# Decay products of a chunk in one scan, tokens and router scores from one matmul, and chunk rows laid six to each eight partitions

## The chip, the core and the metric

The kernel runs on one core of a Trainium2 chip. Such a core has a matrix engine (TensorE, PE in the profile, with its weight load PEld in a row of its own), a vector engine (VectorE, DVE), an activation engine (ScalarE, ACT), a general engine (GpSimd, POOL) and an engine that only issues transfers (SyncE, SP). They run side by side and wait for each other through semaphores. Each works through its own instructions in the order in which the program lists them, so an instruction that waits holds up everything behind it on its engine. Data lies in 128 partitions of on-chip memory. Matmul results land in a second memory, PSUM. Sixteen DMA engines carry data between DRAM and the chip.

The metric is device time in microseconds (us). The kernel before the change took 320.49 us, the median of three runs (319.43 to 320.95).

## What is computed

Two stages follow each other. The first is linear attention with a decay (RWKV) over 4 batches of 8 heads, 768 tokens and 48 features a head; the second is a mixture of 8 experts over the 3072 rows of 384 values that the first one writes. Every row goes to one expert, and a row whose skip score is not positive stays as it is.

```
for t in range(S):                       # per batch and head, D = 48
    cur = einsum('bhd,bhe->bhde', u * k_t, v_t)
    y_t = einsum('bhd,bhde->bhe', r_t, state + cur)
    state = w_t[..., None] * state + einsum('bhd,bhe->bhde', k_t, v_t)
x = y as (3072, 384)
skip = x @ w_skip > 0 ;  e = argmax(x @ w_gate) ;  g = softmax weight of e
out = x + g * relu(x @ w1[e]) @ w2[e]    # rows with skip, else out = x
```

## The kernel before

The tokens of a batch are cut into 6 chunks of 128, so there are 24 chunks in all (batch outermost). Heads are handled in pairs: partitions 0 to 47 hold the 48 features of an even head, partitions 64 to 111 those of the odd one, and a free axis `a` of length 4 counts the pairs. Partitions 48 to 63 and 112 to 127 hold zeros.

The recurrence is turned into matrix products. For each chunk `prep_scan` makes q, the product of the decays from a token to the chunk's end, by a scan that runs backwards over the tokens (line 261); a scan is an instruction in which each element is made from the one before it, here state = max(w * state, floor). `prep_keys` makes rh, the product from the chunk's start divided by the whole product (a reciprocal on line 271, then forward scans that start from it, line 276), and kq = k * q on POOL (line 274). `prep_reads` makes rp = r * rh on DVE (line 284) and rk = r * k on POOL (line 287). Each kind of scan takes four instructions, one for each head pair, since a new pair has to start afresh.

The matmuls of a chunk are: `intra` transposes kq into kt (line 306) and forms the 128 x 128 scores psA (line 313), which `mask` multiplies by a triangle on DVE (line 319, two instructions); `bonus_sums` and `bonus` give the term with u (lines 328 and 332); `update` adds kt and v to the state in psu (line 341), which `carry` scales and copies on ACT (lines 351 and 356); `outputs` sums the chunk's result in psY, from the masked scores (line 363) and, from the second chunk of a batch on, from the state (line 368); `evict` copies it to xT on ACT (line 373). `rows_out` turns xT into rows of tokens by four transposes (line 379), and makes the 9 router scores by four more matmuls with 9 columns (line 381). `store` copies scores and rows out on ACT (lines 389 and 391) and issues the transfer to `out`.

The main loop goes over steps s = -2 to 24. In step s the chunk s is finished (update, outputs, rows_out), chunk s+1 gets its scores, and chunk s+2 its scans; the rows of chunk s-1 are stored, and the loads of chunk s+4 are issued. Tile order is written out by hand (`manual_schedule`), so the code's order is each engine's order. After 6, 12, 18 and 24 chunks a router pass over the finished rows is spread over the next steps, a few small DVE instructions at a time (`drip`); for the first two passes ACT also makes `hot` tables in three steps (lines 462 and 463, called marks below). Beside that, the first experts' weights are loaded and split into a high and a low part, the high one on ACT (line 106), the low one on POOL (line 266). The second stage starts after the last router pass and is not touched by the change.

A chunk's w, r and k arrive by two transfers of 48 partitions each (line 152), one for each half of the partitions, into one of three buffers; v with tokens along the free axis comes in two more (line 154), and v with tokens in partitions in one (line 159). For the first chunk the host has laid out 128 rows with zeros between the halves, and three transfers bring them (lines 144 to 146). The zeros of the two other buffers are written by DVE (line 203) and POOL (line 215) before the loads are issued.

## Time and profile before

| | |
|---|---|
| median of three runs | 320.49 us (319.43 to 320.95) |
| the profiled execution's own time | 320.93 us |
| its span in the trace | 319.1 us, so 1.8 us lie around it |
| first stage up to the last chunk's copy of psY | about 166 us |
| PE, DVE, ACT, POOL busy | 94%, 76%, 58%, 37% of the span |
| moved by DMA | 60.48 MB |

The trace is of one execution. Its views give, for each instruction, a start in us from the span's start, a duration, and where an engine sat idle before it, what ended the idle time. A row that groups instructions ends with the time the group was busy and the mean duration of one in ns. Durations of instructions that follow each other on one engine overlap by some hundredths of a us, so the distance from one start to the next is a better cost than the duration.

### The profile page before, as it was taken

The page shows a single profiled execution, that of the slowest core. Times are in us where ns is not written, and L with a number is a line of the kernel's source. Part 1 is how long each engine was busy: PE and PEld are TensorE (multiplying, and loading weights), DVE is VectorE, ACT ScalarE, POOL GpSimd, SP SyncE. Part 2 cuts the span into 40 slices and gives each one's busy share as a digit, 9 for nine tenths or more (in the row PEclk, how much of TensorE's full clock was granted, in tenths as well). Part 3 has the DMA queues.
Part 4 walks back from the last instruction along what each step waited for, and adds up shares of the span by engine and source line. Part 5 has one row for each costly group of instructions (what it writes and reads, how often), then busy time and mean ns, then how long its engine had stood idle before and what let it go on. Part 6 is the DMA issues. An engine that isn't in the chain of part 4 may idle for free.

```text
span 319.1 us, 8696 instructions
## 1 busy us (share of the span) xinstructions
PE 299.8 (94%) x3325; PEld 280.0 (88%) x3325; DVE 243.2 (76%) x573; ACT 184.4 (58%) x503; POOL 116.6 (37%) x118
## 2 busy tenths in 40 slices
PE   6399999999999999989999999999999999999991
PEld 2289998889788987979889899999999999999991
DVE  7789899999999999999626369587685949596310
ACT  4327765869876898756734258375573818284200
POOL 7164345655455556543401674311102020101111
PEclk9969999999999999979999999999999999999997
DMA  7999999999899998884410479865656373630000
GB/s 228 243 213 226 176 267 276 267 263 264 219 239 234 267 212 179 189 196 165 128 41 25 122 255 359 285 228 197 230 197 238 129 259 99 243 147 26 8 15 25
DMA packets 23108, 60.48 MB, mean 189 GB/s; under 512 B 4102, under 2 KB 10666, under 8 KB 23056
## 3 DMA queue, kind: packets, MB, share of 16 engines
q1 hardware_dynamic: 20576, 53.69, 61.9%
q0 software_dynamic: 2048, 5.48, 5.1%
q8 instruction: 28, 0.46, 0.6%
q10 hardware_dynamic: 432, 0.66, 0.6%
q14 instruction: 24, 0.20, 0.2%
HBM read 52.76 MB, written 7.86 MB: 190 GB/s over the span
## 4 chain that ended last, share of the span: by engine, by line
PE 76%; DVE 9%; DMA 8%; ACT 2%; issue 1%; POOL 1%; SPq 0%; ACTq 0%; POOLq 0%; DVEq 0%
PE psO L768 7%; PE psO L766 7%; PE psO L767 7%; PE psH L748 6%; PE psH L747 6%; PE psH L746 6%; PE psY L363 6%; PE psB L328 6%; PE psA L313 6%; PE psY L368 5%; DMA wrk<-wrk 4%; PE psH L125 4%; DVE asb L319 3%; PE psX L381 3%; DMA vt<-wrk 3%; PE psT L306 2%
## 5 line engine op out<-in xcount | busy, mean ns | idle before, releaser
L753 ACT ACTIVATE hh<-psH 128x256 fp32r<-128x256 f32 x60 | 23.1, 384 | 55.7 <-PE psH L748 52.4
L710 POOL DMA_INDIRECT out<-fin,ids x16 | 16.9, 1058 | 101.5 <-DVE fin L773 93.3
L748 PE MATMUL psH<-xTh,w1l 128*128 128x256 f32 x168 | 47.5, 283 | 0.0
L747 PE MATMUL psH<-xTl,w1h 128*128 128x256 f32 x168 | 47.5, 283 | 0.0
L746 PE MATMUL psH<-xTh,w1h 128*128 128x256 f32 x168 | 47.5, 283 | 0.0
L276 DVE TENSOR_TENSOR_SCAN rh<-wrk,rh,pss 128x127 f32<-128x127 f32 x96 | 38.1, 459 | 3.6 <-ACT tab L503 1.1
L766 PE MATMUL psO<-w2h,hh 128*128 128x384 f32 x120 | 40.7, 339 | 0.0
L768 PE MATMUL psO<-w2h,hl 128*128 128x384 f32 x120 | 40.1, 334 | 0.0
L767 PE MATMUL psO<-w2l,hh 128*128 128x384 f32 x120 | 40.1, 334 | 0.0
L287 POOL TENSOR_TENSOR rk<-wrk 128x512 f32<-128x512 f32 x24 | 30.6, 1275 | 24.7 <-DVE rp L284 16.6
L274 POOL TENSOR_TENSOR kq<-wrk,q 128x512 f32<-128x512 f32 x24 | 28.3, 1181 | 21.8 <-PE psu L341 7.3
L319 DVE TENSOR_TENSOR asb<-psA,c_sb 128x512 f32<-128x512 f32 x48 | 30.8, 682 | 6.5 <-PE psA L313 6.4
L363 PE MATMUL psY<-asb,v 128*48 128x128 f32 x384 | 26.8, 284 | 8.6 <-DVE psY L332 8.4
L754 DVE SCALAR_TENSOR_TENSOR hl<-psH,hh 128x256 fp32r<-128x256 f32 x60 | 25.2, 420 | 12.5 <-ACT hh L753 12.1
L261 DVE TENSOR_TENSOR_SCAN q<-wrk,pss 128x128 f32<-128x128 f32 x96 | 32.3, 398 | 2.7 <-DMA wrk<-wrk 2.7
L748 PEld LDWEIGHTS psH<-xTh,w1l 128*128 128x128 f32 x168 | 32.2, 192 | 0.0
L747 PEld LDWEIGHTS psH<-xTl,w1h 128*128 128x128 f32 x168 | 32.2, 192 | 0.0
L746 PEld LDWEIGHTS psH<-xTh,w1h 128*128 128x128 f32 x168 | 32.2, 191 | 0.0
L773 DVE SCALAR_TENSOR_TENSOR fin<-psO,gates,xg 128x384 f32<-128x384 f32 x15 | 9.3, 618 | 28.5 <-PE psO L768 28.5
L363 PEld LDWEIGHTS psY<-asb,v 128*48 128x48 f32 x384 | 20.8, 127 | 9.8 <-DVE psY L332 9.7
L95 DVE TENSOR_TENSOR w2l<-r,w2h 128x512 fp32r<-128x512 f32 x42 | 27.8, 687 | 1.0
L328 PE MATMUL psB<-rk,ubk_sb 128*128 128x128 f32 x192 | 28.0, 289 | 0.3 <-POOL rk L287 0.3
(145 smaller groups left out, 682.0 us busy)
## 6 DMA issues: line engine op xcount, KB each, us to landing
r<-w SPq DMA_DIRECT2D x48, 512.0 KB, 5.7
wrk<-wrk SPq DMA_DIRECT2D x46, 288.9 KB, 5.9
v<-vN SPq DMA_DIRECT2D x24, 192.0 KB, 5.6
out<-x SPq DMA_DIRECT2D x24, 192.0 KB, 5.2
vt<-wrk SPq DMA_DIRECT2D x46, 96.0 KB, 5.7
wrk<-wrk SPq DMA_DIRECT2D x1, 258.5 KB, 3.7
wrk<-wrk ACTq DMA_DIRECT2D x1, 256.0 KB, 3.9
wrk<-wrk SPq DMA_DIRECT2D x1, 256.0 KB, 4.5
```

Source lines behind the costliest of these rows:

```text
L261: ins = nc.vector.tensor_tensor_scan(q[:, a, :P][:, ::-1], w4[:, a, :P][:, ::-1], floor.to_broadcast([P, P]), 1.0, op0=ALU.mult, op1=ALU.max)
L276: nc.vector.tensor_tensor_scan(rh[:, a, 1:], wk["w4"][:, a, :P - 1], zero.to_broadcast([P, P - 1]), rh[:, a, 0:1], op0=ALU.mult, op1=ALU.max)
L287: mul = nc.gpsimd.tensor_tensor(rk.rearrange("p a j -> p (a j)"), wk["w"][:, R_OFF:K_OFF], wk["w"][:, K_OFF:V_OFF], op=ALU.mult)
L319: nc.vector.tensor_tensor(s, psa[g], tri.rearrange("p (o j) -> p o j", o=1).to_broadcast([P, NP, P]), op=ALU.mult)
L328: nc.tensor.matmul(wk["psb"][:, a], ubk_sb[:, a], wk["rk"][:, a], start=True, stop=True)
L363: nc.tensor.matmul(psy[64 * g:64 * g + D, a], v[:, 2 * a + g], wk["asb"][g][:, a], start=False, stop=(c == 0), skip_group_check=True)
L746: nc.tensor.matmul(ps, w1h[:, o:o + P], xTh[:, kc], start=(kc == 0), stop=False)
L747: nc.tensor.matmul(ps, w1h[:, o:o + P], xTl[:, kc], start=False, stop=False)
L748: nc.tensor.matmul(ps, w1l[:, o:o + P], xTh[:, kc], start=False, stop=(kc == KC - 1))
L766: nc.tensor.matmul(pso, h[j, fc][0], w2h[:, o], start=(fc == 0), stop=False)
L767: nc.tensor.matmul(pso, h[j, fc][0], w2l[:, o], start=False, stop=False)
L768: nc.tensor.matmul(pso, h[j, fc][1], w2h[:, o], start=False, stop=(fc == FC - 1))
```

## The change

**Layout.** A chunk's 48 rows of a head half now lie six to each eight partitions. One transfer brings all 128 partitions: its source pattern takes 16 groups, each six rows further on, and of each group eight rows, so that partitions 6 and 7 of every eight hold a copy of the next group's first two rows. The last chunk, whose last group would read past the array's end, takes two transfers. The copies must not count, so a column `own` (1 in the six, 0 in the two) is made from the identity matrix by a DVE reduction at the start. It scales u (line 255) and the reciprocal rq (line 303, a new ACT instruction in every chunk), and with that the read side rp is zero in those partitions. The clearing of two load buffers goes.

**Whole scans.** q and rh are now one scan of 516 elements each. The four rows of 129 hold a zero decay at the joint, and the scan's second operand is a mask in PSUM (1.0 at the joints, 1e-30 elsewhere, 16-bit values) in place of one broadcast number. rh starts from 1, and the division moves into rp: four DVE instructions (line 316), one for each pair, multiply r, rq and rh, where one instruction multiplied r and rh before.

**Joined output matmul.** The four transposes and four 9-column matmuls of `rows_out` become four matmuls of 105 columns, whose fixed operand holds an identity of 96 columns and the 9 router columns. Their router columns overlap in pairs, so that the scores come as two halves: `store` copies 18 numbers, the rows in two ACT copies of 192 columns in place of one of 384, and the router adds the halves (one more DVE instruction in each pass). The state update's stationary operand grows from 48 to 64 columns.

**Order on POOL.** The low half of a weight slice (line 290 now) was tied to the first scan of the step; it is now tied to the last router instruction that DVE was given, if there was one.

```diff
-            for g in range(2):
-                nc.sync.dma_start(t[64 * g:64 * g + D], wrk[b, c, g, :, :V_OFF])
+            def rows(eng, o, m):
+                if i == n - 1:
+                    src = wrk[b, c].rearrange("g d x -> (g d) x")
+                    pat = [[6 * RW, 15], [RW, 8], [1, m]]
+                    eng.dma_start(t[120:126, o:o + m], src[90:, o:o + m])
+                    p = 120
+                else:
+                    pat, p = [[6 * RW, 16], [RW, 8], [1, m]], P
+                at = wrk[b, c, 0, :, o:o + m]
+                eng.dma_start(t[:p, o:o + m], bass.AP(at.tensor, at.offset, pat))
...
+            rows(nc.sync, 0, V_OFF)
...
-            nc.vector.memset(wrk_sb[1], 0.0)
-            nc.vector.memset(floor, Q_MIN)
-            nc.vector.memset(zero, 0.0)
+            nc.vector.memset(smask, Q_MIN)
+            nc.vector.memset(smask[:, :, 0:1], 1.0)
+            nc.vector.tensor_copy(smaskb, smask.rearrange("p a j -> p (a j)"))
+            nc.vector.tensor_copy(pss[:, 200:200 + NP * CW // 2], smaskb.bitcast(F32))
...
-            nc.gpsimd.memset(wrk_sb[2], 0.0)
...
+            nc.vector.tensor_reduce(own, ident.rearrange("p (i j) -> p i j", j=8)[:, :, :6],
+                                    axis=mybir.AxisListType.XY, op=ALU.add)
...
-            for a in range(NP):
-                ins = nc.vector.tensor_tensor_scan(
-                    q[:, a, :P][:, ::-1], w4[:, a, :P][:, ::-1], floor.to_broadcast([P, P]), 1.0,
-                    op0=ALU.mult, op1=ALU.max)
-                if a == 0 and lows:
-                    lo, raw, hi = lows.pop(0)
-                    beside(nc.gpsimd.tensor_tensor(lo, raw, hi, op=ALU.subtract), ins)
+            if lows:
+                lo, raw, hi = lows.pop(0)
+                mul = nc.gpsimd.tensor_tensor(lo, raw, hi, op=ALU.subtract)
+                if vec.last is not None:
+                    beside(mul, vec.last)
+            nc.vector.tensor_tensor_scan(
+                q.rearrange("p a j -> p (a j)")[:, ::-1], t[:, 1:1 + NP * CW][:, ::-1], floor, 0.0,
+                op0=ALU.mult, op1=ALU.max)
...
-            nc.vector.reciprocal(rh[:, :, 0:1], wk["q"][:, :, 0:1])
+            nc.vector.reciprocal(rq0, wk["q"][:, :, 0:1])
+            nc.scalar.activation(rq, rq0, AF.Copy, scale=own)
...
-            for a in range(NP):
-                nc.vector.tensor_tensor_scan(
-                    rh[:, a, 1:], wk["w4"][:, a, :P - 1], zero.to_broadcast([P, P - 1]),
-                    rh[:, a, 0:1], op0=ALU.mult, op1=ALU.max)
+            nc.vector.tensor_tensor_scan(
+                rh.rearrange("p a j -> p (a j)"), wk["w"][:, 0:NP * CW], floor, 0.0,
+                op0=ALU.mult, op1=ALU.max)
...
-            last = nc.vector.tensor_tensor(rp, wk["r"], rh, op=ALU.mult)
+            for a in range(NP):
+                last = nc.vector.scalar_tensor_tensor(
+                    rp[:, a], wk["r"][:, a], wk["rq"][:, a], wk["rh"][:, a, :P],
+                    op0=ALU.mult, op1=ALU.mult)
...
             for a in range(NP):
-                nc.tensor.transpose(psx[:, a, :LO], xT[:LO, a], ident[:LO, :LO])
-            for a in range(NP):
-                nc.tensor.matmul(psx[:, NP - 1, LO:LO + E + 1], xT[:, a], wgp_sb[:, a, 2 * D:],
-                                 start=(a == 0), stop=(a == NP - 1))
+                o = (a // 2) * X2 + (a % 2) * 2 * D
+                nc.tensor.matmul(px[:, o:o + XW], xT[:, a], wgp_sb[:, a], start=(a == 0),
+                                 stop=(a == NP - 1), skip_group_check=True)
...
-            nc.scalar.copy(x, psx.rearrange("p a (g d) -> p a g d", g=2)[:, :, :, :D])
+            for o in range(2):
+                nc.scalar.copy(x[:, o::2].rearrange("p h g d -> p h (g d)"),
+                               p2[:, :, o * XW:o * XW + 2 * D])
...
+            vec.tensor_tensor(lg, l2[:, :, 0], l2[:, :, 1], op=ALU.add)
```

Three places show how instructions stand now. The first is DVE in a step of the first batch, from the scans of chunk 3 to the bonus of chunk 2 (a scan is printed as SCALAR_TENSOR_TENSOR; the numbers behind a name count buffers). Before:

```order
L261 SCALAR_TENSOR_TENSOR q_117<-wrk_83,pss 128x128 x4
L271 RECIPROCAL rh_391<-q_117 128x4
L276 SCALAR_TENSOR_TENSOR rh_391<-wrk_83,rh_391,pss 128x127 x4
L284 TENSOR_TENSOR rp_399<-wrk_83,rh_391 128x512
L319 TENSOR_TENSOR asb_2_428<-psA_108,c_sb 128x512
L319 TENSOR_TENSOR asb_2_430<-psA_109,c_sb 128x512
L332 TENSOR_TENSOR psY<-psB_432,vt_88 128x512
```

And the same place on DVE in the changed kernel:

```order
L294 SCALAR_TENSOR_TENSOR q_375<-wrk_83,pss 128x516
L302 RECIPROCAL rq_390<-q_375 128x4
L308 SCALAR_TENSOR_TENSOR rh_395<-wrk_83,pss 128x516
L316 SCALAR_TENSOR_TENSOR rp_397<-wrk_83,rq_389,rh_395 128x128 x4
L353 TENSOR_TENSOR asb_2_429<-psA_112,c_sb 128x512
L353 TENSOR_TENSOR asb_2_431<-psA_113,c_sb 128x512
L366 TENSOR_TENSOR psY<-psB_433,vt_88 128x512
```

Eight scans became two and one product became four; the four read rq_389, which ACT writes.

The second place is ACT in a step of that batch: the stored rows, the state's carry, and the copies behind them. Before:

```order
L389 COPY lgs_356<-psX_441 128x9
L391 COPY x_457<-psX_441 128x384
L351 ACTIVATE psu<-psu,q_117 128x48 x4
L356 COPY sblk_111<-psu 64x4x48 x2
L373 COPY xT_502<-psY 128x512
L308 COPY kt_509<-psT_504 128x512
```

And ACT there in the changed kernel:

```order
L424 COPY lgs_355<-psX_442 128x18
L427 COPY x_453<-psX_442 128x2x96 x2
L385 ACTIVATE psu<-psu,q_375 128x48 x4
L390 COPY sblk_115<-psu 64x4x48 x2
L303 ACTIVATE rq_485<-rq_486,own 128x4
L407 COPY xT_500<-psY 128x512
L342 COPY kt_507<-psT_502 128x512
```

The new rq stands behind the whole carry, and the copy of the rows is in two parts.

The third place is DVE at the program's start, ahead of the first chunk's scans. Before:

```order
L208 MEMSET q_117 128x4
L210 MEMSET psA_108 128x512
L210 MEMSET psA_109 128x512
L261 SCALAR_TENSOR_TENSOR q_116<-wrk_83,pss 128x128 x4
L271 RECIPROCAL rh_182<-q_116 128x4
```

And in the changed kernel:

```order
L237 COPY pss<-smaskb 128x258
L239 MEMSET psA_112 128x512
L239 MEMSET psA_113 128x512
L251 TENSOR_REDUCE own<-c_sb 128x1
L294 SCALAR_TENSOR_TENSOR q_181<-wrk_83,pss 128x516
L302 RECIPROCAL rq_184<-q_181 128x4
```

The reduction that makes `own` reads the constants c_sb and stands ahead of the first scan.

More of the change, by code (lines that the diff above doesn't have):

```diff
@@ L46 @@
 XW = 2 * D + E + 1
+X2 = XW + 2 * D
 BIG = 65536.0
@@ L166, in rwkv_moe_kernel @@
         u_sb = keep.tile([P, NP], F32, name="u_sb")
+        u8_sb = pers.tile([P, NP], F32, name="u8_sb")
+        own = pers.tile([P, 1], F32, name="own")
         ident = c_sb[:, C_ID:C_ID + P]
@@ L191, in rwkv_moe_kernel, with __getattr__, issue @@
         pr = pss[:, :NC * E].rearrange("p (c e) -> p c e", e=E)
-        floor = pss[:, 500:501]
-        zero = pss[:, 501:502]
+        floor = pss[:, 200:200 + NP * CW // 2].bitcast(BF16)
         pt = pss[:, 64:64 + 2 * NV * E].rearrange("p (j q e) -> p j q e", j=2, q=NV)
-        qs = [pers.tile([P, NP, CW], F32, name=f"q{i}") for i in range(2)]
+        class Steps:
+            last = None
+            def __getattr__(self, name):
+                def issue(*a, **kw):
+                    self.last = getattr(nc.vector, name)(*a, **kw)
+                    return self.last
+                return issue
+        vec = Steps()
         def setup():
@@ L340, in update @@
                 for g in range(2):
-                    nc.tensor.matmul(psu[64 * g:64 * g + D, a, :D],
-                                     work[i]["kt"][:, a, 64 * g:64 * g + D],
+                    nc.tensor.matmul(psu[64 * g:64 * g + HP, a, :D],
+                                     work[i]["kt"][:, a, 64 * g:64 * g + HP],
                                      v_sb[i][:, 2 * a + g, :D],
@@ L432, in router @@
             sm = t("sm", 1)
-            nc.vector.tensor_reduce(sm, ex, axis=AX, op=ALU.add)
+            vec.tensor_reduce(sm, ex, axis=AX, op=ALU.add)
             yield 1
-            nc.vector.tensor_scalar(sm, sm, 1e-9, None, op0=ALU.add)
+            vec.tensor_scalar(sm, sm, 1e-9, None, op0=ALU.add)
             yield 1
             gate = t("gate", 1)
-            nc.vector.reciprocal(gate, sm)
+            vec.reciprocal(gate, sm)
             vals = att.tile([P, NC, NV, 1], BF16, tag="vals", name=f"vals{i0}")[:, :m]
@@ L466, in router @@
             last = i0 + m == n
-            small = nc.vector if last else nc.gpsimd
+            small = vec if last else nc.gpsimd
             for c in range(m):
@@ L525, in early @@
             yield 1
-            nc.vector.tensor_reduce(gate0, tab[:, 0, 2:NV, 0], axis=AX, op=ALU.add)
+            vec.tensor_reduce(gate0, tab[:, 0, 2:NV, 0], axis=AX, op=ALU.add)
             yield 1
@@ L686, in rwkv_moe_kernel @@
         psf = ps1.tile([P, 512], F32, tag="psT", name="psf", bufs=2)
-        nc.tensor.matmul(psf[0:1, 0:1], rows1, vt[:, 0:1], start=True, stop=False)
+        nc.tensor.matmul(psf[0:1, 0:1], rows1_, vt[:, 0:1], start=True, stop=False)
         nc.tensor.matmul(psf[0:1, 0:1], rows1_, vt[:, 2:3], start=False, stop=True)
```

70 lines of the change are left out of this document (39 added, 31 removed).

## The prediction

> **What bounds the kernel now.** I read the slices first, then the chain of work, then the instructions of two steps in order of time. In the 40 slices of 8 us the two engines that matter are these:
>
> ```profile
> PE   6399999999999999989999999999999999999991
> DVE  7789899999999999999626369587685949596310
> ```
>
> The first stage fills slices 1 to 21, and there both stand at 9. From about 168 us on PE alone is full, and the change touches nothing there. So two engines run close together, and which of them ends last has to be read step by step. The chain has this step in the first batch:
>
> ```profile
> 36.18 0.49 PE psu L341 x16
> 36.68 0.88 PE psY L363 x16
> 37.55 1.09 PE psY L368 x8
> 38.64 0.44 PE psT L306 x4
> 39.08 1.02 PE psA L313 x24
> 40.10 1.09 PE psB L328 x8
> 41.19 0.38 PE psX L379 x4
> 41.57 0.81 PE psX L381 x8
> ```
>
> The parts add to 6.20 us with no gap: PE is the bound in these steps, some six of them up to 54 us. Later the router's small instructions come on DVE and the marks on ACT. This is DVE over one later step, by starts, and the busy time in two stretches:
>
> ```profile
> 67.17 1.34 DVE L261 TENSOR_TENSOR_SCAN q<-wrk,pss 128x128 f32<-128x128 f32 x4
> 68.55 0.18 DVE L271 RECIPROCAL rh<-q 128x4 f32<-128x4 f32 x1
> 68.77 1.59 DVE L276 TENSOR_TENSOR_SCAN rh<-wrk,rh,pss 128x127 f32<-128x127 f32 x4
> 70.39 0.69 DVE L284 TENSOR_TENSOR rp<-wrk,rh 128x512 f32<-128x512 f32 x1
> 71.00 1.28 DVE L319 TENSOR_TENSOR asb<-psA,c_sb 128x512 f32<-128x512 f32 x2
> 72.20 0.69 DVE L332 TENSOR_TENSOR psY<-psB,vt 128x512 f32<-128x512 f32 x1
> 72.80 1.35 DVE L261 TENSOR_TENSOR_SCAN q<-wrk,pss 128x128 f32<-128x128 f32 x4
> ...
> core 0: us, PE busy (x) PEld busy (x) DVE busy (x) ACT busy (x) POOL busy (x), PEclk, DMA share, GB/s
> ...
> 70.00:80.00 10.00, 10.00 (x162) 9.26 (x157) 9.86 (x22) 9.71 (x28) 5.53 (x7) 1.00 1.03 256
> ...
> 130.00:140.00 10.00, 8.95 (x134) 7.86 (x135) 9.68 (x30) 6.62 (x22) 4.74 (x5) 0.88 0.75 172
> ```
>
> One chunk costs DVE 1.38 + 0.22 + 1.62 + 0.61 + 1.20 + 0.60 = 5.63 us from the first row to the last, and router instructions come on top. So from 54 us on DVE is the bound in the router's steps, and in the steps with marks (70 to 80) ACT is as full as DVE.
>
> **PE: the joined matmul.** Lines 379 and 381 take 0.38 + 0.81 = 1.19 us. Four matmuls with the same stationary size and 105 columns lie between the 0.81 us of four with 9 columns and the 1.09 us of four with 128 (line 328). By the columns between these ends that is 0.81 + 96/119 x 0.28 = 1.04, so PE saves 0.15 us a step (bounds 0.10 and 0.38). The wider stationary operand of line 341 (64 columns for 48) I cost at nothing, since 16 instructions in 0.49 us are 31 ns each and the 64-column ones of line 313 cost no more than 1.02/24 = 43 ns; at worst 16 x 12 ns = 0.19 us.
>
> **DVE: scans against products.** The mean durations of the groups:
>
> ```profile
> L276 DVE TENSOR_TENSOR_SCAN rh<-wrk,rh,pss 128x127 f32<-128x127 f32 x96 | 38.1, 459 | 3.6 <-ACT tab L503 1.1
> L754 DVE SCALAR_TENSOR_TENSOR hl<-psH,hh 128x256 fp32r<-128x256 f32 x60 | 25.2, 420 | 12.5 <-ACT hh L753 12.1
> L773 DVE SCALAR_TENSOR_TENSOR fin<-psO,gates,xg 128x384 f32<-128x384 f32 x15 | 9.3, 618 | 28.5 <-PE psO L768 28.5
> L261 DVE TENSOR_TENSOR_SCAN q<-wrk,pss 128x128 f32<-128x128 f32 x96 | 32.3, 398 | 2.7 <-DMA wrk<-wrk 2.7
> ```
>
> No scan of 516 is in the trace. From below: a DVE instruction on 4 elements takes 0.18 us (line 271 above), so a scan's slope is at least (398 - 181)/124 = 1.75 ns an element, and 516 take 1.08 us. From above: no fixed part at all, and the whole scan costs what the four do, 1.38. I take 1.19, nearer to the lower end because a fixed part is seen in every short row. That saves 0.19 us on q and 1.62 - 1.19 = 0.43 on rh (bounds 0 to 0.30, and 0.24 to 0.54). The mask as second operand costs nothing here: the old floor was read from PSUM as well.
>
> Against this, rp becomes four products with a factor per partition. Such a factor costs 459 - 398 = 61 ns in the scans. With it line 773 takes 618 ns for 384, without it line 754 takes 420 for 256, so the slope is (618 - 61 - 420)/128 = 1.07 ns, and 128 elements with a factor take 420 - 137 + 61 = 344 ns. Of that some 0.08 overlaps with the next (0.69 lasts, 0.61 to the next start), so four take 1.05 us where one took 0.61: 0.44 more. The bounds are 0 (four pack as closely as one) and 4 x 0.344 - 0.61 = 0.77 (no overlap). Together DVE saves 0.19 + 0.43 - 0.44 = **0.18 us a chunk** (bounds 0.84 saved and 0.53 lost). The addition of the score halves costs 0.2 in each router pass.
>
> **ACT and the new wait.** rp now waits for rq from ACT, where it stands behind the carry. In a step with marks:
>
> ```profile
> 74.26 0.48 ACT L391 COPY x<-psX 128x384 f32<-128x384 f32 x1
> ...
> 74.63 1.20 ACT L351 ACTIVATE psu<-psu,q 128x48 f32<-128x48 f32 x4
> ...
> 75.61 1.18 POOL L274 TENSOR_TENSOR kq<-wrk,q 128x512 f32<-128x512 f32 x1
> ...
> 75.86 0.64 ACT L356 COPY sblk<-psu 64x192 f32<-64x192 f32 x2
> 76.02 1.31 DVE L284 TENSOR_TENSOR rp<-wrk,rh 128x512 f32<-128x512 f32 x1
> ...
> 77.25 1.28 DVE L319 TENSOR_TENSOR asb<-psA,c_sb 128x512 f32<-128x512 f32 x2
> ```
>
> The carry ends at 76.50. rq lasts 0.19 at most (as the reciprocal does on DVE), and the split copy costs between nothing more and 0.64 - 0.37 = 0.27 (the two 192-element copies of line 356, against 74.63 - 74.26); I take 0.08. With two such copies and one earlier rq ahead of it, rq is done near 76.95. rp then takes 1.05 and ends at 78.0, where today the next instruction starts at 77.25 (rp lasts 1.31 there, through the end of kq on POOL). So such a step loses 0.75 us, and behind rp the masks, the bonus and PE's line 363 are queued. A second such step adds 0.2 by the same drift: 0.95 for a batch, two batches with marks, **1.9 us lost**. In the PE-bound steps the wait is covered: psA, which the masks need, ends at 40.10, which is 3.9 us after psu begins, and carry, rq and rp together (0.5 for the store, 1.2, 0.64, 0.2, 1.05) end 3.6 after it. If that cover went, masks would come late by the difference.
>
> **Start.**
>
> ```profile
> 1.18 0.45 ACTq L147 DMA_DIRECT2D c_sb<-cst  x1
> ...
> 4.52 1.36 DVE L261 TENSOR_TENSOR_SCAN q<-wrk,pss 128x128 f32<-128x128 f32 x4 [0.60 <-DMA wrk<-wrk]
> ...
> 10.67 1.36 DVE L261 TENSOR_TENSOR_SCAN q<-wrk,pss 128x128 f32<-128x128 f32 x4 [2.09 <-DMA wrk<-wrk]
> ...
> 16.45 0.88 PE L363 MATMUL psY<-asb,v 128*48 128x128 f32 x6 [4.96 <-DVE psY L332]
> ...
> c_sb<-cst ACTq DMA_DIRECT2D x1, 128.0 KB, 4.7
> ```
>
> `own` makes the first scan wait for c_sb, until 1.18 + 4.7 = 5.9, and takes some 0.3: the scan starts 1.7 us later. The idle 2.09 us ahead of the second chunk's scan covers it. From there to PE's first psY it is 5.78 us now, and 1.19 + 0.22 + 1.19 + 1.05 + 1.80 = 5.45 then, and chunk 1 may land sooner without the cleared buffer. I take 0.6 us gained (bounds 1.0 lost, 0.9 gained).
>
> **The sum**, against the profiled execution's 320.93 us: start -0.6; six PE-bound steps x 0.15 = -0.9; about ten chunks under DVE x 0.18 less three additions of 0.2 = -1.2; marks +1.9; three PE-bound steps near 150 us -0.45. The last router pass gains 0.15 from the shorter psX and loses 0.2. That is -1.25, or 319.7; the median lies 0.44 below that execution, so **319.2 us**.
>
> **Rivals.** *Transfers become the bound (slower).* One chunk's w, r and k grow by a third, from 577.8 to 770.4 KB.
>
> ```profile
> r<-w SPq DMA_DIRECT2D x48, 512.0 KB, 5.7
> wrk<-wrk SPq DMA_DIRECT2D x46, 288.9 KB, 5.9
> ```
>
> The DMA share is 1.03 already at 256 GB/s, so at today's rate 192.6 KB cost 0.75 us a chunk; over 17 chunks 12.8. The loads are issued two steps (12.4 us) ahead and land in 5.9, which swallows 6.5. The rest, 6.3, would show: 327. It decides once a chunk's transfers take longer than the 6.2 us step. Against it speaks that 512 KB to 128 partitions land as fast as 288.9 KB to 48, so the wide transfer should move a byte faster. Chance 0.10.
>
> The Trainium skill (DMA: Bandwidth & Descriptors, "The descriptor swizzle") says that in a full 128-partition transfer each DMA engine writes partitions of a port of its own, four and four. With a source of 16 groups of eight, an engine might get eight neighbours instead and share ports two by two; by that rule the byte would move no faster than now, and the time would be the 327. No run here shows it.
>
> *PE's clock drops more often.* The row of 130 to 140 us grants 0.88, that is 1.2 us lost, behind this wait:
>
> ```profile
> 137.12 1.45 PE L363 MATMUL psY<-asb,v 128*48 128x128 f32 x16 [1.05 <-DVE psY L332]
> ```
>
> Those matmuls take 1.45 where 0.88 is usual. PE has less work after the change, and longer gaps in the marks' steps; two more drops cost 2.4 or more: 321.6 to 322.8. Chance 0.10.
>
> The Trainium skill (TensorE: Matmul & The Clock Gate, "Part 1: The HAM clock gate") asks for an idle window of about 3.4 us before the clock halves. By that no gap here would do it and this rival would cost nothing; the trace shows a drop behind a gap of 1.05 us, and the measurement decides.
>
> *More is gained.* The four products pack to 0.8 us and ACT hides rq: 0.4 a chunk, marks lose 0.3 a batch. Then 0.6 + 0.9 + 4.0 - 0.6 - 0.6 + 0.45 = 4.75, 315.7; without the present clock drop 314.5. For it: ACT waits in most steps, and DVE's order gives rq the whole rh scan. Chance 0.25.
>
> *The whole scan saves nothing.* At 1.38 each, DVE loses 0.2 a chunk and the marks 0.2 more a batch: 0.6 + 0.9 - 2.0 - 0.6 - 2.3 + 0.45 = 2.95 lost, 323.4. Chance 0.10.
>
> **The numbers.** The forecast has 0.45 and a range of its own from 317.6 to 320.9. A measurement of this kernel tells about 0.5% (1.6 us) from no change. Faster by more: 0.17 of the forecast and the 0.25, 0.42. Within: 0.27 of the forecast, most of the clock rival and a little of the last, 0.36. Slower: 0.22. From 314.5 to 322.8 some 0.2 is left out: the transfers, half of the last rival, a little of the gain.
>
> **What would show it.** Right: a scan of 516 near 1.2 us, four products near 1.05 from first start to mask, psX near 1.04, six early steps of 6.05 us, DVE waiting for ACT rq ahead of rp in the marks' steps. Wrong: wide loads that land later than 6 us and DVE waiting for them; products under 0.8 us; scans near 1.08 or 1.38; granted clock under 1 in more stretches than the two at 10 to 30 us and the one at 130 to 150.

## The result: 3% slower, and the profile after

| | before | after |
|---|---|---|
| median | 320.06 us (4 runs, 319.43 to 320.95) | 329.79 us (4 runs, 328.68 to 331.03) |
| ratio to before, 95% interval | | 1.0303, 1.0247 to 1.0359 |
| span of the profiled execution | 319.1 us | 326.6 us |
| moved by DMA | 60.48 MB | 64.97 MB |

So 9.7 us are lost where 1.25 were forecast to be gained. After the first four experiments every kernel, that of before too, took 7 to 10 us longer in most of its executions (before: 331 us), by the traces in the second stage, which the change does not touch, so times are compared inside one call only, and for the first stage the traces are read.

The 40 slices after, PE, DVE and the DMA share in tenths:

```profile
PE   6779998998898799889999999999999999999993
DVE  6799799996799786999954477859494958677320
...
DMA  7999999999999999998611159975736463650001
```

PE and DVE, which stood at 9 nearly throughout the first stage, now show many a 7 and 8 there, and DMA stands at 9 from the second slice to the eighteenth. One window over the middle of the first stage says it in numbers. The columns are the window and its length, the busy time of PE, PE's weight loads, DVE, ACT and POOL, the granted clock, the share of the 16 DMA engines and GB/s. Before:

```profile
20.00:140.00 120.00, 116.53 (x1774) 104.83 (x1769) 113.02 (x283) 88.67 (x272) 63.22 (x56) 0.98 0.97 231
```

And after:

```profile
20.00:140.00 120.00, 108.47 (x1596) 94.85 (x1596) 103.35 (x209) 89.23 (x288) 60.33 (x55) 0.97 1.04 251
```

PE and DVE each have some 8 to 10 us less of work in these 120, and the DMA engines went from nearly full to full. The transfers' own rows (KB each, median us from issue to landing):

```profile
r<-w SPq DMA_DIRECT2D x48, 512.0 KB, 6.2
wrk<-wrk SPq DMA_DIRECT2D x22, 770.5 KB, 10.3
out<-x SPq DMA_DIRECT2D x24, 192.0 KB, 7.0
```

A chunk's w, r and k now land 10.3 us after their issue, where the halves took 5.9. (A KB of the profile is 1024 bytes.) What that does to the engines, the waits of the first stage tell (engine, line, releaser: total us, times, longest):

```profile
DVE rp L316 <- ACT rq L303: 12.6, 12, 1.9
...
ACT x L427 <- DMA out<-x: 6.2, 7, 1.6
...
ACT w1h L107 <- DMA r<-w: 3.6, 1, 3.6
...
ACT w2h L107 <- DMA r<-w: 3.4, 1, 3.4
```

ACT, which waited for no transfer in the steady part of the first stage before, waits 13.2 us for transfers, and DVE waits 12.6 us for ACT. One step in order of time shows how the two hang together (start, duration, engine, line, and idle time with its releaser):

```profile
76.97 1.23 DVE L294 TENSOR_TENSOR_SCAN q<-wrk,pss 128x516 f32<-128x516 f32 x1 [1.30 <-DMA wrk<-wrk]
...
78.78 0.54 ACT L427 COPY x<-psX 128x192 f32<-128x192 f32 x2 [1.63 <-DMA out<-x]
79.21 1.22 ACT L385 ACTIVATE psu<-psu,q 128x48 f32<-128x48 f32 x4
80.46 0.64 ACT L390 COPY sblk<-psu 64x192 f32<-64x192 f32 x2
81.12 0.30 ACT L303 ACTIVATE rq<-rq,own 128x4 f32<-128x4 f32 x1
...
81.45 1.14 DVE L316 SCALAR_TENSOR_TENSOR rp<-wrk,rq,rh 128x128 f32<-128x128 f32 x4 [1.92 <-ACT rq L303]
...
82.08 1.14 PE L415 MATMUL psX<-wgp_sb,xT 128*128 128x105 f32 x8 [1.64 <-ACT xT L407]
...
84.45 1.95 PE L397 MATMUL psY<-asb,v 128*48 128x128 f32 x16 [0.63 <-DVE psY L366]
```

DVE's scan waits for a wide load itself, the only such wait behind the start in this trace. An earlier chunk's rows have not left yet, so ACT cannot write the buffer; the carry, rq and xT stand behind it; DVE's rp and PE's psX wait for those; and after the gap PE's line 397 takes 1.95 us where some 1.08 is usual, at a lower clock (granted 0.57 from 84.4 to 88.1 us).

The durations themselves came out close to the forecast:

```profile
L316 DVE SCALAR_TENSOR_TENSOR rp<-wrk,rq,rh 128x128 f32<-128x128 f32 x96 | 30.4, 378 | 13.0 <-ACT rq L303 12.6
...
L294 DVE TENSOR_TENSOR_SCAN q<-wrk,pss 128x516 f32<-128x516 f32 x24 | 29.3, 1219 | 2.7 <-DMA wrk<-wrk 2.6
L308 DVE TENSOR_TENSOR_SCAN rh<-wrk,pss 128x516 f32<-128x516 f32 x24 | 28.9, 1205 | 2.7 <-PE pss L535 1.3
```

### The profile page after: what moved, and what is told of

Its sections match the earlier page's. It is cut to its first block, busy times and chain, and to the rows that moved or that the text cites. A ratio compares the mean times of both kernels' runs of the same rounds, so it can differ in the third digit from the quotient of the medians.

```text
span 326.6 us, 8417 instructions
## 1 busy us (share of the span) xinstructions
PE 299.2 (92%) x3229; PEld 275.4 (84%) x3229; DVE 242.1 (74%) x505; ACT 192.6 (59%) x551; POOL 115.2 (35%) x117
## 2 busy tenths in 40 slices
DMA packets 24292, 64.97 MB, mean 199 GB/s; under 512 B 4683, under 2 KB 11119, under 8 KB 24243
## 4 chain that ended last, share of the span: by engine, by line
PE 62%; DMA 21%; DVE 7%; issue 3%; POOL 2%; ACT 2%; SPq 1%; POOLq 0%; DVEq 0%; ACTq 0%
DMA r<-w 7%; PE psO L807 6%; PE psO L809 6%; PE psO L808 6%; PE psH L789 6%; PE psH L788 6%; PE psH L787 6%; DMA vt<-wrk 6%; DMA wrk<-wrk 6%; PE psY L397 4%; PE psY L402 4%; PE psA L347 4%; PE psB L362 4%; PE psH L126 3%; DVE asb L353 3%
## 5 line engine op out<-in xcount | busy, mean ns | idle before, releaser
L316 DVE SCALAR_TENSOR_TENSOR rp<-wrk,rq,rh 128x128 f32<-128x128 f32 x96 | 30.4, 378 | 13.0 <-ACT rq L303 12.6
L397 PE MATMUL psY<-asb,v 128*48 128x128 f32 x384 | 27.6, 289 | 12.9 <-DVE psY L366 12.9
L294 DVE TENSOR_TENSOR_SCAN q<-wrk,pss 128x516 f32<-128x516 f32 x24 | 29.3, 1219 | 2.7 <-DMA wrk<-wrk 2.6
L308 DVE TENSOR_TENSOR_SCAN rh<-wrk,pss 128x516 f32<-128x516 f32 x24 | 28.9, 1205 | 2.7 <-PE pss L535 1.3
L415 PE MATMUL psX<-wgp_sb,xT 128*128 128x105 f32 x192 | 25.4, 275 | 3.8 <-ACT xT L407 3.8
## 6 DMA issues: line engine op xcount, KB each, us to landing
wrk<-wrk SPq DMA_DIRECT2D x22, 770.5 KB, 10.3
```

The lines of the kernel that those rows point to most:

```text
L294: nc.vector.tensor_tensor_scan(q.rearrange("p a j -> p (a j)")[:, ::-1], t[:, 1:1 + NP * CW][:, ::-1], floor, 0.0, op0=ALU.mult, op1=ALU.max)
L308: nc.vector.tensor_tensor_scan(rh.rearrange("p a j -> p (a j)"), wk["w"][:, 0:NP * CW], floor, 0.0, op0=ALU.mult, op1=ALU.max)
L316: last = nc.vector.scalar_tensor_tensor(rp[:, a], wk["r"][:, a], wk["rq"][:, a], wk["rh"][:, a, :P], op0=ALU.mult, op1=ALU.mult)
L397: nc.tensor.matmul(psy[64 * g:64 * g + D, a], v[:, 2 * a + g], wk["asb"][g][:, a], start=False, stop=(c == 0), skip_group_check=True)
```

## The experiments

Two theories. **T**: the transfers are the bound where weights are loaded beside the wide chunks. **R**: the new wait of rp for ACT's rq is the loss. Both have the waits above for them, since a late transfer makes ACT late and ACT makes rq late.

### One cause at a time

These four ran on one chip, where before took 320.99 us. The changed kernel itself did not run in that call. Its loss was 9.7 us (3.0%) in the first measurement and 6.35 us (1.9%, by medians) in a later call, so what a version "brings back" is known only between these two.

*Old loads.* `narrow` gives a chunk two transfers of 48 partitions again:

```diff
-            rows(nc.sync, 0, V_OFF)
+            for g in range(2):
+                nc.sync.dma_start(t[64 * g:64 * g + D], wrk[b, c, g, :, :V_OFF])
...
-            nc.vector.tensor_reduce(own, ident.rearrange("p (i j) -> p i j", j=8)[:, :, :6],
+            nc.vector.tensor_reduce(own, ident.rearrange("p (i j) -> p i j", j=8),
```

The two buffers are cleared again, and u comes in one transfer. In this version the bias of the `hot` tables is 0 in place of 1 in 32 of the 128 partitions, which leaves some routing entries wrong, with the same instructions; `q_narrow` below has the right bias.

> The change with the loads of before: a chunk's w, r, k in two transfers of 48 partitions (577.8 KB, no copies), two buffers cleared at the start, own all ones; whole scans, rq on ACT and the joined matmuls stay. Theory T (the transfers are the bound in the first stage: 770 + 576 + 512 KB = 1858 KB in a step with weights, 7.3 us at 256 GB/s, against a step of 6.0): back under before, 316 to 320 us, DVE's wait for ACT's rq shrinks to under 5 us of the 12.6, and ACT no longer waits for the rows' transfers. Theory R (the loss is the new wait of rp for rq, which stands on ACT behind the store and the carry; the late transfers only happen beside it): 326 us or more, and the wait for rq stays near 12 us.

Measured: 323.66 us median, ratio 1.0066 (1.0036 to 1.0096), in neither range. In the trace, which is that of the longest of eight executions (326.83 us), DVE's wait for rq is 10.4 us; ACT's 4.1 us of waiting for the rows' transfers there do not come back in the trace of `q_narrow`. Neither theory does alone: without the wide loads the kernel loses less than half as much, and yet it does not come back under before.

*Weights later.* `late` changes two of four starting steps:

```diff
-                for eq, k0 in (((0, 1), 0), ((0, 0), 3), ((1, 0), 8), ((1, 1), 16)):
+                for eq, k0 in (((0, 1), 0), ((0, 0), 16), ((1, 0), 8), ((1, 1), 19)):
```

> The change with the loads of the first expert's first weights (3 x 512 KB) moved from steps 6 to 8 to steps 19 to 21, and those of the second expert's second weights from there to steps 22 to 24, so that 1.5 MB less (6 us of transfer time at 256 GB/s) lie ahead of step 19; nothing else is changed. Theory T: the losses of steps 6 to 10 and 13 shrink, 324 to 327 us. Theory R: no difference within 1 us, 329 to 331.

Measured: 325.29 us, 1.0128 (1.0074 to 1.0182). That is inside T's range: with the wide loads kept and every instruction as it was, moving 1.5 MB to later steps brings back something, between a third and over half of the loss, by which of the two measurements of the changed kernel it is held against. Its trace does not settle it: the copy of the last chunk's psY starts at 172.0 us, against 174.8 and 171.7 in two traces of the changed kernel. `mask_late` below is the clean form of this test.

*Bytes alone.* `dummy` is the kernel before with 192.6 KB more per chunk:

```diff
+            nc.sync.dma_start(spare, wrk[b, c, 0, :32, :V_OFF])
```

> The kernel before, with one more transfer in each of 23 chunks: 32 rows of 6020 bytes (192.6 KB) to a buffer that nobody reads, issued behind the chunk's w, r, k. The result is computed in full. Theory T: the bytes alone cost what the change lost, and there is no gain of the engines to set against it: 327 to 333 us. Theory R, or a cost of the wide pattern rather than of its bytes: 320 to 322.

Measured: 331.55 us, 1.0342 (1.0307 to 1.0377). T: as many bytes in an ordinary transfer to 32 partitions cost 10.6 us, in a kernel that has none of the change's new waits. (A row has 6164 bytes, not the 6020 of the expectation; 32 of them are the 192.6 KB.) One more issue a chunk on SyncE's queue goes with the bytes. In the trace, which is that of the quickest of four executions (328.04 us), the last chunk's copy comes 6.8 us later than before, and 2.5 of that lie ahead of the second chunk's copy.

*rq on DVE.* `rqdve` was meant to take ACT out of rp's way:

```diff
-            nc.scalar.activation(rq, rq0, AF.Copy, scale=own)
+            nc.vector.tensor_scalar(rq.rearrange("p a o -> p (a o)"), rq0.rearrange("p a o -> p (a o)"), own, None, op0=ALU.mult)
```

> The change with rq scaled by own on DVE (one more instruction of 128x4 in each chunk) and not on ACT; the wide loads stay. Theory T: the steps are paced by transfers, so the 12.6 us of DVE's waits for rq turn up at other waits (PE for xT, ACT for the rows' buffers and weights): 327 to 331 us. Theory R: rp no longer waits for ACT: 318 to 322 us.

Measured: 334.48 us, 1.0409 (1.0389 to 1.0428), above both ranges. The experiment does not tell, because the edit brought a cost of its own. The trace of `rqdve` in one step, DVE and POOL:

```profile
33.18 0.18 DVE L302 RECIPROCAL rq<-q 128x4 f32<-128x4 f32 x1
33.40 1.09 DVE L303 TENSOR_SCALAR rq<-rq,own 128x4 f32<-128x4 f32 x1
34.40 1.22 DVE L308 TENSOR_TENSOR_SCAN rh<-wrk,pss 128x516 f32<-128x516 f32 x1
...
33.28 1.18 POOL L306 TENSOR_TENSOR kq<-wrk,q 128x512 f32<-128x512 f32 x1 [1.62 <-PE psY L397]
```

An instruction on four elements takes 1.09 us, until POOL's kq is through. A scan beside kq is not prolonged; this is one in the changed kernel:

```profile
78.33 1.20 DVE L308 TENSOR_TENSOR_SCAN rh<-wrk,pss 128x516 f32<-128x516 f32 x1
...
78.39 1.17 POOL L306 TENSOR_TENSOR kq<-wrk,q 128x512 f32<-128x512 f32 x1
```

The Trainium skill (SBUF — State Buffer, "Who interferes with whom") says that a DVE `tensor_scalar` in its two-port mode and a GpSimd instruction take one port pair in turn, and that a DVE instruction with one SBUF input outside that mode does not contend. The rows agree with both, though they do not show which mode was used.

### Both causes, taken out cleanly

To take rq off ACT without a new instruction there are two ways. With old loads nothing has to be scaled (`narrow_direct`: rp reads the reciprocal). With wide loads `own` can go into the joints of the scans' mask (`wide_mask`): in the partitions with copies both scans then fall to the floor of 1e-30, and kq is next to nothing there.

```diff
-            nc.vector.reciprocal(rq0, wk["q"][:, :, 0:1])
-            nc.scalar.activation(rq, rq0, AF.Copy, scale=own)
+            nc.vector.reciprocal(rq, wk["q"][:, :, 0:1])
...
+            nc.vector.tensor_copy(smaskb.rearrange("p (a j) -> p a j", a=NP)[:, :, 0:1],
+                                  own.rearrange("p (a o) -> p a o", o=1).to_broadcast([P, NP, 1]))
```

(The last two lines are in `wide_mask` alone, at the start; it also clears the mask as 16-bit values at once.) Four runs in one call, before at 331.49 us. The ranges in the expectations were set for a before of 320.5, so they are read here as ratios to it:

> The change with the loads of before (two transfers of 48 partitions, no copies), and with no scaling of rq: the products read the reciprocal that DVE wrote, and ACT has no rq. Theory R2 (with the bytes gone, what is left of the loss is rp's wait for ACT, 10 us of DVE's waiting in the run with rq on ACT): 317 to 319.5 us. Theory S (what is left is the start, 2 us, and ACT itself late behind the rows' transfers, which rp's wait only shows): 321 to 323.

Measured: 328.16 us, 0.9899 (0.9877 to 0.9921). R2 (0.989 to 0.997): without the wide loads, the wait for rq was the rest of the loss, and this version is 1% faster than before.

> The change with its wide loads, and with own written into the joints of the scans' mask (0 in the partitions with copies, so that both scans fall to the floor there and kq is zero), in place of the scaling of rq on ACT: the result is computed in full, rp waits for no engine but its own. Theory T (transfers are the bound): 326 to 330 us. Theory R (the wait for ACT's rq is what costs): 318 to 322.

Measured: 336.62 us, 1.0146 (1.0119 to 1.0174). That is nearer to T (1.017 to 1.030) than to R (up to 1.005), in neither range, and some 2.5% over `narrow_direct`, which differs by the wide loads and what goes with them.

*The wide load alone*, in the kernel before:

> The kernel before with the wide loads alone: 770.4 KB to 128 partitions in one transfer, no cleared buffers, u and the first column of rh scaled by own, the state update with 64 columns. Old scans, old output matmuls. (The scaling of that column is one more instruction on DVE in each chunk, beside kq on POOL, which took 0.95 us where the change's rq was scaled so: about 10 us of DVE, not all on the path.) Theory T: 329 to 336 us, as slow as or slower than the same bytes in a transfer of their own. A cost of other parts of the change: 321 to 324.

Measured: 346.29 us, 1.0440 (1.0411 to 1.0469). T again; the scaling on DVE is in it, and its share was not separated.

*More mended at once.* `best` is `narrow_direct` with the mask cleared as 16-bit values, nothing made of `own`, and three buffers for the rows:

```diff
-            nc.vector.memset(smask, Q_MIN)
-            nc.vector.memset(smask[:, :, 0:1], 1.0)
-            nc.vector.tensor_copy(smaskb, smask.rearrange("p a j -> p (a j)"))
+            nc.vector.memset(smaskb, Q_MIN)
+            nc.vector.memset(smaskb.rearrange("p (a j) -> p a j", a=NP)[:, :, 0:1], 1.0)
...
-            x = att.tile([P, NP, 2, D], F32, tag="x", name=f"x{i}")
+            x = att.tile([P, NP, 2, D], F32, tag="x", name=f"x{i}", bufs=3)
```

> As with old loads and no rq on ACT, and further: the mask is written as 16-bit values at once (no cast, which took 2.7 us beside POOL's clearing), nothing is made of own, and the stored rows have three buffers in place of two, so that ACT's copy waits less for the rows' transfer. Theory R2: 314 to 317 us. Theory S: 317 to 320, since the start and the rows' buffers are mended here and the wait for ACT's rq was only a sign.

Measured: 328.54 us, 0.9904 (0.9879 to 0.9928), the same as `narrow_direct`. Read alone, the number lies in S's range (0.989 to 0.998) and misses R2's. But S had `narrow_direct` above before and a gain of 3 to 4 us from there to `best`, and neither came: with the old loads neither that part of the start nor the rows' buffers bind.

### Do the two add?

The same four combinations on one chip, before at 330.79 us (median of 11).

> The changed kernel, once more, on the same chip as the next three, which remove the wide loads, the scaling of rq on ACT, or both. Theory A (the two costs add, since the bytes delay one set of steps and the wait for rq another): against before it is slower by the sum of both. From ratios on different chips so far: wide loads 2.4%, rq on ACT 1.6%, the rest of the change a gain of 1%, so 1.030. Theory O (they overlap: a step that is paced by transfers has room for the wait): each removed alone brings under half of what both bring.

> The change with the loads of before, rq on ACT; otherwise as the first such run, but the result is computed in full (there, a wrong bias in 32 of 128 partitions spoilt some routing entries, with the same instructions), and the four load transfers stand in the order of before. Theory A: 1.006 of before, 2.4% under the changed kernel. Theory O: within 1.2% of the changed kernel.

> The change with its wide loads, own in the joints of the mask, no rq on ACT, on the chip of the others. Theory A: 1.014 of before, 1.6% under the changed kernel. Theory O: within 0.7% of the changed kernel.

> The change with the loads of before and no rq on ACT, on the chip of the others: 0.990 of before again by both theories; by A its distance from the changed kernel is the sum of the two single ones, by O it is more than the sum.

| median, us | rq on ACT | no rq on ACT |
|---|---|---|
| wide loads | 337.14 | 337.34 |
| old loads | 333.02 | 327.82 |

The ratios with their intervals are `q_after` 1.0393 (1.0340 to 1.0447), `q_narrow` 1.0266 (1.0214 to 1.0318), `q_mask` 1.0403 (1.0313 to 1.0492), `q_direct` 0.9945 (0.9730 to 1.0161). They go by two of the eleven executions of before (323.9 and 324.67 us), and the first three set medians with the longer second stage against these, so medians of all executions are compared here, and the first stage in the traces.

Theory O, and plainly: with wide loads it makes no difference that shows whether rp waits for ACT (+0.2, where `q_mask` scatters from 335.7 to 338.9); with old loads that wait costs 5.2 us. Taking out the wide loads brings 4.1 us with rq on ACT and 9.5 without. Each cause hides behind the other, so a test that removes one of them underrates it. (A's 1.006 for `q_narrow` came true, its 1.014 for `q_mask` did not.) The traces say the same without the second stage. The row of the 24 copies of psY to xT ends with the start of the first and of the last, which is the end of the first stage. The changed kernel, old loads, mask, and both, in this order:

```profile
L407 ACT COPY xT<-psY x24: 585/586/588, 20.1 to 171.7; 128x512 f32<-128x512 f32 x24
```

```profile
L393 ACT COPY xT<-psY x24: 586/586/588, 19.0 to 169.1; 128x512 f32<-128x512 f32 x24
```

```profile
L405 ACT COPY xT<-psY x24: 586/586/612, 19.7 to 174.1; 128x512 f32<-128x512 f32 x24
```

```profile
L391 ACT COPY xT<-psY x24: 585/585/588, 18.9 to 164.2; 128x512 f32<-128x512 f32 x24
```

Before, it went from 18.5 to 166.1. So the wide loads cost 2.6 us by these ends with rq on ACT and 9.9 without. Two traces of the changed kernel differ by 3.1 us here (174.8 in `after`), two without either cause by 0.2 (164.0 in `narrow_direct`), so a difference of some 3 us between single traces with wide loads tells nothing. Between such starts the stretches below were taken (us; chunks are counted from 0, and the first row goes from the start of the span to the copy of chunk 1):

| from start to start | before | after | `q_after` | `q_narrow` | `q_mask` | `q_direct` |
|---|---|---|---|---|---|---|
| span's start to 1 | 26.3 | 27.9 | 28.3 | 26.2 | 28.0 | 25.7 |
| 1 to 8 | 43.7 | 44.8 | 43.8 | 43.1 | 46.7 | 42.8 |
| 8 to 10, marks | 13.1 | 16.0 | 14.0 | 13.9 | 14.6 | 13.2 |
| 10 to 14 | 24.9 | 28.0 | 27.6 | 25.9 | 27.6 | 25.3 |
| 14 to 18, marks | 24.8 | 26.0 | 26.0 | 27.9 | 24.8 | 24.8 |
| 18 to 23 | 33.4 | 32.1 | 32.1 | 32.1 | 32.4 | 32.4 |

With wide loads (`q_mask`) the loss sits up to chunk 14, in the start and in the steps that load weights; with rq on ACT (`q_narrow`) it sits for the most part at the marks and behind them. The steps of chunks 19 to 23 are faster in all four.

How the two late sides look when only one is there: in `q_mask` ACT waits, but no longer in front of rp, and DVE waits for the wide loads themselves.

```profile
ACT x L425 <- DMA out<-x: 10.6, 8, 3.0
...
DVE q L294 <- DMA wrk<-wrk: 5.4, 5, 1.9
```

In `q_narrow` ACT has no gap at all in the marks' steps, and its new instruction is simply more work there:

```profile
74.02 1.22 ACT L371 ACTIVATE psu<-psu,q 128x48 f32<-128x48 f32 x4
75.27 0.64 ACT L376 COPY sblk<-psu 64x192 f32<-64x192 f32 x2
75.93 0.30 ACT L289 ACTIVATE rq<-rq,own 128x4 f32<-128x4 f32 x1
76.25 0.59 ACT L393 COPY xT<-psY 128x512 f32<-128x512 f32 x1
```

From rq's start to the next it is 0.32 us, which is what such a step lost against `q_direct` (13.9 to 13.2 for two). The largest single piece lies behind the second marks, in this execution (in both traces of the changed kernel and in `narrow` the step of chunk 17 takes 5.21 us, here 6.72):

```profile
122.98 1.14 DVE L302 SCALAR_TENSOR_TENSOR rp<-wrk,rq,rh 128x128 f32<-128x128 f32 x4 [1.50 <-ACT rq L289]
...
125.98 1.67 PE L383 MATMUL psY<-asb,v 128*48 128x128 f32 x16 [1.23 <-DVE psY L352]
127.58 2.08 PE L388 MATMUL psY<-rp,sblk 128*128 128x128 f32 x8
```

DVE came late by 1.50 us of waiting for rq, PE stood still for 1.23 us, and the next two groups took 3.75 us instead of about 2.2: the clock (granted 0.55 from 125.98 to 129.45 us). Against `q_direct` the steps of chunks 17 and 18 lost 2.5 us.

### What was still open

Three more, before at 331.44 us.

> Wide loads, own in the joints of the mask (no rq on ACT), and the weights' loads moved as in the run with late weights: 1.5 MB later. Theory O (the transfers bind where weights are loaded beside wide chunks, the wait for rq binds elsewhere, and each hides the other): both are gone here, so 0.985 to 0.995 of before, as with old loads and no rq. If the wide pattern costs by itself: 1.005 or more.

Measured: 332.06 us, 1.0018 (0.9997 to 1.0038), between the two. The place of the weights is all that differs from `wide_mask` and `q_mask`, which stood 5.1 and 6.6 us over before; here it is 0.6. By the trace the first stage is 7.3 us shorter than that of `q_mask` (166.8 against 174.1). Its stretches from chunk 1 to 8 (43.3), 8 to 10 (13.2), 10 to 14 (25.3) and 14 to 18 (24.8) are those of `q_direct` within 0.6 us: with the weights out of the way, the wide loads cost next to nothing per step. What stays is the start: the copy of chunk 1 starts at 27.8, against 25.0 in the next run. Part of it is this, in the trace of `mask_late`:

```profile
12.21 1.23 DVE L294 TENSOR_TENSOR_SCAN q<-wrk,pss 128x516 f32<-128x516 f32 x1 [1.00 <-DMA wrk<-wrk]
```

> Old loads, no rq on ACT, and the late weights. Theory O, with nothing left of the transfers' bound: the same ratio as without late weights, 0.990, within 0.4%. If transfers still hold some steps there: 0.980 to 0.986.

Measured: 328.35 us, 0.9905 (0.9877 to 0.9934). As O expects: without the extra bytes, moving the weights gains nothing.

*The start.* `start_u` issues u's three transfers on ACT's queue:

```diff
-                nc.sync.dma_start(u_sb, uP)
+                nc.scalar.dma_start(u_sb, uP)
...
-                    nc.sync.dma_start(u8_sb[64 * g:64 * g + HP],
+                    nc.scalar.dma_start(u8_sb[64 * g:64 * g + HP],
```

> The changed kernel with the three transfers of u issued on ACT's queue, behind v of the first chunk, in place of SyncE's: the second chunk's load is issued some 2 us earlier (at 5.67 us now). Theory O: the second chunk's scan starts over 1 us earlier and its row copy with it, but steps that wait for transfers swallow part of that: 0.3 to 1.5 us faster than the changed kernel (1.030 to 1.039 of before by chip). If the start is hidden altogether: no difference.

Measured: 338.68 us, 1.0199 (1.0157 to 1.0240). The changed kernel is not in this call, and with 1.030 and 1.019 in two others the ratio does not tell a gain. The trace does: the copy of chunk 1 starts at 30.1 us, against 27.9 and 28.3 in the changed kernel, so the start became longer. The second chunk's load did go out at 3.00 us, but u came late, and this is what followed in its trace:

```profile
12.53 1.07 ACT L255 ACTIVATE ubk_sb<-u_sb,own 64x256 f32<-64x256 f32 x2 [4.01 <-DMA u_sb<-uP]
13.62 0.30 ACT L303 ACTIVATE rq<-rq,own 128x4 f32<-128x4 f32 x1
...
13.96 0.35 DVE L316 SCALAR_TENSOR_TENSOR rp<-wrk,rq,rh 128x128 f32<-128x128 f32 x1 [4.86 <-ACT rq L303]
```

The first rq stands behind the two instructions that make ubk, and these wait for u. So the run traded one delay for a longer one and leaves open what the order on SyncE's queue alone costs.

## Why the prediction was wrong

**The durations of the engines' work: right where an instruction runs alone.** Scans of 516 take 1.22 and 1.21 us (taken: 1.19). The four products take 1.06 us from first start to mask (81.45 to 82.51 in the trace after; taken: 1.05). Early steps went from 6.20 to 5.99 us in `q_direct` (0.21 saved; forecast 0.15), and the start in that kernel gained 0.6 (25.7 against 26.3; forecast 0.6). The steps of chunks 19 to 23 gained 1.0 (33.4 to 32.4; forecast 0.45 for three of them), which is luck: 0.87 of it is the step of chunk 19, where the gap of 1.05 us and its clock drop are gone (7.91 us before, 7.04 in `q_direct`), and the four others gained 0.13 together. With only these parts of the change the kernel is 1.0% faster than before, 3.3 us by medians; by the trace 1.9 us of that lie in the first stage, and where the rest lies is open.

**The step that failed first: transfers at nothing.** The sum had no term for them; it was the rival with 0.10, and the argument against it was that "512 KB to 128 partitions land as fast as 288.9 KB to 48, so the wide transfer should move a byte faster". A landing time is that of a transfer that runs beside others, and does not say what sixteen full engines do with more bytes. The view that did say it was quoted too: a share of 1.03 at 256 GB/s. After the change the share is 1.04 over 120 us at 251 GB/s, and `dummy` shows that an ordinary transfer of the 192.6 KB costs about as much. In its place the runs showed 9.5 us for the wide loads without rq on ACT and 4.1 with it. The rival's own working came close in part by luck: it gave 327 for what became 329.8, from the bytes, rate and lead, but the measured loss also holds the wait for rq and the start. What it lacked is where the bytes meet: the 512 KB of weights of nine of the first fourteen steps. There a step moves 770 + 192 + 192 + 192 + 512 = 1858 KB, an estimate of 7.6 us at 251 GB/s, against a step of 6; elsewhere 1346 KB, 5.5 us. `mask_late` shows it: with three of these nine loads moved behind step 18, the loss against before shrinks by 4.5 to 6 us (by medians; 7.3 in the first stage of the traces). The prediction's own sign for this case, wide loads that land later than 6 us, came with 10.3.

Does the wide pattern move a byte faster, as the prediction had it? The main queue before and after (packets, MB, share of 16 engines over spans of 319.1 and 326.6 us):

```profile
q1 hardware_dynamic: 20576, 53.69, 61.9%
...
q1 hardware_dynamic: 21763, 58.21, 65.3%
```

That is 3.68 and 3.66 us of all sixteen engines for one MB, and 3.69 in `dummy`. By the single transfer records of the traces, a row of w, r and k (6164 bytes) took 449 ns on average before, 442 in `dummy` and 411 in the wide load: 8% less time for a row, against a third more rows. So by these records it is the bytes that cost and not the pattern, and what the pattern gains is far from paying for them. Which partitions an engine wrote, on which the prediction's use of the Trainium skill (DMA: Bandwidth & Descriptors, "The descriptor swizzle") rests, no trace here shows.

**The second step that failed: the wait for rq, charged at the marks alone.** 1.9 us were charged, all at the marks, and "in the PE-bound steps the wait is covered". With old loads the wait cost 5.2 us by medians. By the traces it is 4.9 us at the end of the first stage (169.1 against 164.2). Of these the four marks' steps have 1.3, 0.32 each, as much as ACT's added work, which the term held at "rq lasts 0.19 at most" (it lasts 0.30). The rest came where nothing was charged: 2.5 us behind one gap that lowered PE's clock, and 1.1 in the start and the router's other steps. The drop behind that gap is in this trace and not in those of the changed kernel, and how often it comes is not known. The rival on the clock had named such drops, at 2.4 for two; in the changed kernel one stands behind the late transfers (line 397 at 84.45 above), so it was no rival but a part. The Trainium skill's idle window for the clock (TensorE: Matmul & The Clock Gate, "Part 1: The HAM clock gate") of about 3.4 us does not agree with the trace of `q_narrow`: the drop stands behind a gap of 1.23 us.

**The third step that failed: the 1.2 us to be gained in the steps under DVE.** From chunk 8 to chunk 18 `q_direct` takes 63.3 us and the kernel before 62.8, though DVE was to save 0.18 a chunk there. In the steps with marks the four products now run beside POOL's kq (`q_direct`):

```profile
73.88 2.17 DVE L300 SCALAR_TENSOR_TENSOR rp<-wrk,rq,rh 128x128 f32<-128x128 f32 x4
...
74.14 1.24 POOL L290 TENSOR_TENSOR kq<-wrk,q 128x512 f32<-128x512 f32 x1
```

From the first product to the mask it is 2.08 to 2.19 us in the four steps where all of kq falls into that time, and 1.05 in the three steps behind each pair of them. Before, the one product beside kq took 1.23 to 1.51 in these steps. The prediction quoted that row (1.31, "through the end of kq on POOL") and still put the four at 1.05. In `q_narrow`, where rp waits for rq until kq is through, they take 1.05 to 1.06 in the same steps, so there the wait for rq replaces this loss and does not add to it.

**The start: right in size, but for the loads.** The forecast of 0.6 gained holds with the old loads. With the wide ones the copy of chunk 1 came 1.6 us later: the working let chunk 1 land "sooner without the cleared buffer", but its load was issued at 5.67 us, behind two more small transfers for u, and is a third longer. SyncE's queue before, and after:

```profile
2.60 2.35 SPq L152 DMA_DIRECT2D wrk<-wrk  x2
```

```profile
2.37 0.59 SPq L162 DMA_DIRECT2D u_sb<-uP  x1
3.00 1.39 SPq L165 DMA_DIRECT2D u_sb<-uP  x2
4.69 0.34 SPq L176 DMA_DIRECT2D v<-vN  x1
5.67 0.58 SPq L155 DMA_DIRECT2D wrk<-wrk  x1
```

**The sum, mended.** By the medians of the call with the four combinations: -3.0 for the engines' work and the start, +5.2 for rq on ACT, and then +4.1 for the wide loads. They add to the 6.35 us by which the changed kernel stood over before there, since each is the difference of two neighbours; this is a division of the loss and no check of it. The two costs may not be read off singly: in the other order they are +9.5 and -0.2. Why the first measurement had 9.7 is open; 3.1 us of scatter show between the two traces of the changed kernel in the first stage alone. (Two slips in the recorded working change nothing: its items come to 1.20 with the last router pass, not 1.25, and 192.6 KB take 0.77 us at 256 GB/s, not 0.75.)

## What to carry to other kernels

When the DMA share stands at 1 in a stretch, price added bytes by the rate of that stretch, step by step against the step's length, and not by landing times. When instructions become shorter, look at what they now run beside: the four products lost by POOL's kq what the scans had gained. A small instruction on a lightly used engine costs what stands in front of it on that engine's queue, so look at the stretches in which that engine is full. Where two suspects show up in the same waits, run all four combinations, the changed kernel among them in the same call: here one of them alone seemed to cost nothing.

## Hardware that was not expected

*A tiny DVE instruction that takes 1 us.* The `tensor_scalar` on four elements beside POOL's kq, above: 953 ns on average in `rqdve`, where the reciprocal on as many elements takes 178.

*Waits that the profile does not explain.* The same kernel took 320.94 to 329.0 us over 12 executions. Two profiles of it, from `q_direct` (320.94 us) and `narrow_direct` (328.19 us), run alike up to 177 us; behind the flag at the end of the router DVE shows this in the one

```profile
181.56 0.42 DVE L779 SCALAR_TENSOR_TENSOR hl<-psH,hh 128x256 fp32r<-128x256 f32 x1 [0.98 <-issue]
```

and this in the other:

```profile
186.51 0.42 DVE L779 SCALAR_TENSOR_TENSOR hl<-psH,hh 128x256 fp32r<-128x256 f32 x1 [5.93 <-issue]
```

It is the second such instruction in both, and "issue" means that the profile shows nothing that it waited for. But it starts 0.42 us behind ACT's hh (line 778) in both, and in the second trace that hh waited 6.24 us for PE's line 730. The delay is on PE, in the first trace and in the second:

```profile
182.70 0.82 PE L730 MATMUL psX<-c_sb,xg 128*128 128x128 f32 x6
```

```profile
183.19 0.38 PE L730 MATMUL psX<-c_sb,xg 128*128 128x128 f32 x2 [0.63 <-issue]
184.62 0.60 PE L730 MATMUL psX<-c_sb,xg 128*128 128x128 f32 x4 [1.05 <-issue]
```

PE stands still between two matmuls of one group, and goes on so in the groups behind. What it waits for there is open.
